# One pool for the eight PSUM banks, score halves placed on their own, and new lists for three engines

## The chip, the core and the metric

The kernel runs on one core of one Trainium2 chip. The metric is the device time of one execution in microseconds (us). Each kernel is built once and run several times; one more execution is profiled, and its rows are what this document reads. TensorE is called PE, VectorE DVE, ScalarE ACT, GpSimd POOL and SyncE SP, as in the profile. PE writes only to PSUM, which has eight banks of 512 fp32 values per partition; ACT and DVE read it.

## The reference

The input is q, k and v with 8 batches, 8 heads, 576 positions and 64 values per head. An attention with a window of 128 positions and a linear position bias feeds a channel mix.

```python
scores = scale * np.matmul(q, k.transpose(0, 1, 3, 2))
rel = pos[:, None] - pos[None, :]
mask = (rel >= 0) & (rel < window)                       # window = 128
scores = np.where(mask, scores + bias[None], -1e9)       # bias = -slope[head] * |rel|
attn = exp(scores - max) ; attn /= attn.sum(-1)
x = (attn @ v) as [8, 576, 512]                          # heads side by side
x_prev = x shifted by one position
xk = mu_k * x + (1 - mu_k) * x_prev
xr = mu_r * x + (1 - mu_r) * x_prev
k = np.maximum(xk @ w_k, 0.0)                            # 512 -> 1024
v = k * k @ w_v                                          # 1024 -> 512
out = sigmoid(xr @ w_r) * v
```

## The kernel before

The work is cut into blocks, one block being a run of instructions on one engine. For a batch and a pair of heads these are, in the order of the data:

- q and k are turned (transposes in `qk_quad` L1078, `halves` L837, or by a DMA), and copied from PSUM to `qk` (L696).
- `scores` (L698) multiplies k by q for the blocks that the window touches (L726, 12 matmuls with 64 rows of the array). A head pair fills two halves, `HALF0` and `HALF1`, of 2 x 512 values each. ACT takes the exponential of each half (L740) into `at`, and DVE multiplies by the mask and bias factors (L753). For the first batch the bias is added by matmuls instead (L713).
- `attend` (L759) multiplies by v (L781, 18 matmuls), DVE takes a reciprocal (L787) and scales into `xu` (L793).
- `out_t` or `out_some` turn `xu` back (L820, L837), ACT copies it to `xt` (L696), and `shift` makes xk and xr on DVE (L880, L887).

The channel mix works on pairs of batches (1152 rows) in pieces of 256 to 512 rows. For each of eight column groups a K block (L983, four matmuls) makes xk @ w_k, ACT applies relu (L990), DVE or ACT squares (L964, L962). For each 128 rows an R block (L1001, four matmuls) makes xr @ w_r, ACT takes tanh (L1008), two V blocks (L1017, four matmuls each) make the last product, DVE combines both (L1022), and SP sends the row out (L1047).

PSUM is held in six tiles. Two tiles `duo` have two banks each (class `p2`), and four tiles `uno` have one bank each (class `p1`). The two halves of a head pair's scores take the two duos together; an attend takes one duo; everything else takes an uno. A `Hold` is a claim on a buffer of a class; it is taken when a block starts in the plan and given back when its last reader has ended.

The order is not left to a scheduler. `Plan.add` collects all blocks with their dependences; the lists in `ORDER` say for PE, ACT and DVE in which order each runs its blocks, and `Plan.run` (L161) goes through the lists, hands out the buffers and emits the instructions in the order of its own start times. Below it, the tile layer puts in the semaphore waits: for every tile it keeps the order of emission between a write and the reads and writes of the same tile that conflict with it. `Plan.pick` (L130) chooses the buffer: the lowest free one for a class without pairs; for a class with pairs, a single claim takes a free bank whose partner is in use if there is one:

```python
return max(free, key=lambda a: ((a ^ 1) not in free, a))
```

Of the kernel before, what the change touches and what calls it, by code (L numbers as in the profile page):

```python
# [38 lines left out]
""".split()],  # L39
    "ACT": [int(x) for x in """  # L40
# [11 lines left out]
""".split()],  # L52
    "DVE": [int(x) for x in """
# [187 lines left out]
def kernel(  # L241
# [25 lines left out]
    W = D + 1  # L267
# [30 lines left out]
    SS = ()  # L298
# [70 lines left out]
    duo = [pst.tile([128, 2, 512], FP32, name=f"duo{i}") for i in range(2)]  # L369
    uno = [pst.tile([128, 512], FP32, name=f"uno{i}") for i in range(4)]  # L370
    N1 = 4
    PT = "p1"

    def one(h):
        return uno[h.idx if h.cls == "p1" else N1 + h.idx]

    def two(h):
        return duo[h.idx]

    plan = Plan(dict(qx=2, p2=2, p1=N1, pt=4 - N1, qk=NQ, at=NA, xu=NX, vs=NV, cb=NC, ts=2, tt=2, xt=2, dl=2, dl0=4,  # L380
                     xk=2, rl=3, kk=3, rs=4, ot=NO),
                {}, WAIT)
# [291 lines left out]
    h_mu = Hold("p1")  # L674
# [9 lines left out]
    h_wm = Hold("p1")  # L684
# [13 lines left out]
    def scores(b, g, parts, bias, hq, ha, deps, prio, need, free):  # L698

        todo, dur = [], 0.0  # L700
        for (pieces, m0, tt) in parts:
            a0 = BASE[pieces[0][0]] + pieces[0][1] - 128 * pieces[0][0]
            w = sum(n for _, _, n in pieces)
            todo.append((pieces, m0, tt, a0, w, Hold("p2")))
            dur += sum(max(n / 2400 + .0025, .03) for _, _, n in pieces)
            dur += 0.01 + (2 * mm(w) if bias else 0)
# [24 lines left out]
        s = op(PE, (0.12 if bias else 0.02) + dur, deps, prio + (2,), emit, list(need) + [x[5] for x in todo], free)  # L731
# [27 lines left out]
    def attend(b, g, t0, t1, ha, deps, prio):  # L759
# [3 lines left out]
        hp, hx = Hold("p1" if 2 * nt * W <= 512 else "p2"), Hold("xu")  # L763
# [5 lines left out]
        def a5():  # L769
            if hp.cls == "p1":  # L770
                return one(hp)[:, 0:2 * nt * W].rearrange("p (h t c) -> p h t c", h=2, c=W)
            return two(hp)[:, :, 0:nt * W].rearrange("p h (t c) -> p h t c", c=W)
# [36 lines left out]
    def out_t(b, g, t0, t1, hx, deps, prio, hk, ht, late=None):  # L809

        c0, c1 = 128 * t0, min(S, 128 * t1)
        n = c1 - c0
        hp = Hold(PT if b else "p1")

        def tp():
            return one(hp).bitcast(BF16)

        def emit(e):
            for t in range(t0, t1):
                nc.tensor.transpose(  # L820
                    tp()[:, 128 * t:128 * t + 128],
                    xu_buf[hx.idx][:, t].rearrange("p h d -> p (h d)"), ident)

        o = op(PE, 0.0565 * (t1 - t0), deps, prio + (1,), emit, [hp], [hx])
        x = op(XT(b, g), {ACT: act_t(n), DVE: dve_t(n)}, [o, virt_xt[b]], prio + (1,), lambda e: copy_any(
            e, xt_buf[ht.idx][:, g, X0 + c0:X0 + c1], tp()[:, c0:c1]), (), [hp])
        return shift(b, g, c0, c1, [x], prio, hk, ht, late)

    def halves(n, block):

        hp = [Hold("p1"), Hold("p1")]
# [75 lines left out]
    def tails_full(b, prio, htt, hs):  # L907
        hp = Hold("p1")
# [16 lines left out]
    def tails(b, prio):  # L925
# [8 lines left out]
        hp = Hold("p1")  # L934
# [33 lines left out]
    def channel_mix(P, c0, c1, first, xks, xrs, order):  # L968
# [9 lines left out]
        for fo in range(NFO):  # L978
            hp, hr = Hold("p1"), Hold("rl")
# [16 lines left out]
        for i, c in enumerate(range(c0 // 128, c1 // 128)):  # L996
            hp, hs = Hold("p1"), Hold("rs")
# [12 lines left out]
            hv, ho = Hold("p1"), Hold("ot")  # L1010
# [16 lines left out]
            for a, b in ((0, FIN), (FIN, 512)) if final else ((0, 512),):  # L1027
                if a:
                    hv = Hold("p1")
# [40 lines left out]
    def qk_quad(b, g, nr, buf, deps, prio, c0, hq, take, free):  # L1070

        hp = [Hold("p1"), Hold("p1")]
# [25 lines left out]
    for part in range(2):  # L1098
# [3 lines left out]
        for g in range(G):  # L1102
# [13 lines left out]
            hp = Hold("p1") if part == 0 else None  # L1116
# [51 lines left out]
    def mask_pe(j):  # L1168
        hp = Hold("p2")
# [55 lines left out]
    def qk_full(b, g, prio):  # L1225
        hp, hq = Hold(PT), Hold("qk")
# [101 lines left out]
```

## Time and profile before

| | before |
|---|---|
| median of 3 runs | 229.33 us (228.99 to 229.42) |
| the profiled execution's own time | 228.84 us |
| its span (first to last instruction) | 227.1 us |
| PE busy | 221.8 us (98% of the span), 2587 matmuls |
| DVE busy | 188.8 us (83%) |
| ACT busy | 155.0 us (68%) |
| POOL busy | 92.0 us (41%) |
| mean granted clock of PE | 0.998 |

The profile's page lists the busy time of each engine, the span in 40 slices with the busy tenths of each engine and the granted clock, the chain of work that ended last, and groups of equal instructions. In a group's row the number after the comma is the mean duration of one instruction in ns, and "idle before" is how long its engine stood idle just ahead of such instructions, with what released it. Durations of matmuls overlap: the next one starts well before the one before it has drained.

### The profile page before, as it was taken

How to read it: one execution, taken by the hardware profiler on the slowest of the kernel's cores; microseconds unless marked ns; L12 is line 12 of the kernel's file. 1: busy time of each engine (PE TensorE's matmuls, PEld its weight loads, DVE VectorE, ACT ScalarE, POOL GpSimd, SP SyncE). 2: the span in 40 equal slices, each digit the busy share in tenths (PEclk: the TensorE clock that was granted, in tenths of full speed). 3: DMA queues.
4: the chain of work that ended last, by engine and by line, in shares of the span. 5: the costliest groups of instructions: out<-in, count | busy, mean ns of one | idle time of the engine just before them, and what ended most of it. 6: DMA issues, size and time to landing. Idle time of an engine off the chain costs nothing.

```text
span 227.1 us, 6442 instructions
## 1 busy us (share of the span) xinstructions
PE 221.8 (98%) x2587; PEld 133.2 (59%) x2587; DVE 188.8 (83%) x423; ACT 155.0 (68%) x279; POOL 92.0 (41%) x118
## 2 busy tenths in 40 slices
PE   8899999999999999999999999999999999999994
PEld 8576766755666755556666554546765455446552
DVE  6786999899879998899978996999899988963433
ACT  0678999999989984975868358768567564047511
POOL 8856726599962964385208750240000000000000
PEclk9999999999999999999999999999999999999999
DMA  6999999999999999999999999999150415430124
GB/s 165 179 185 200 197 196 175 199 180 151 196 156 165 137 130 180 168 182 147 211 180 158 120 185 231 177 136 222 30 135 3 123 46 52 131 136 3 49 92 139
DMA packets 129981, 33.19 MB, mean 146 GB/s; under 512 B 116632, under 2 KB 126112, under 8 KB 129952
## 3 DMA queue, kind: packets, MB, share of 16 engines
q0 software_dynamic: 95728, 16.26, 97.5%
q1 hardware_dynamic: 32480, 15.94, 34.1%
q10 hardware_dynamic: 1744, 0.59, 1.1%
q8 instruction: 20, 0.33, 0.6%
q14 instruction: 9, 0.07, 0.1%
HBM read 33.56 MB, written 9.44 MB: 189 GB/s over the span
## 4 chain that ended last, share of the span: by engine, by line
PE 92%; ACT 3%; DMA 2%; SPq 1%; issue 0%; DVE 0%; DVEq 0%; ACTq 0%
PE uno L983 28%; PE uno L1017 28%; PE uno L1001 13%; PE duo L726 7%; PE duo L781 7%; DMA qx<-in_q_dram 2%; PE uno L837 2%; PE uno L1078 2%; ACT at L740 1%; PE duo L713 1%; ACT qk L696 1%; PE uno L781 1%; SPq L550 1%; PE uno L687 1%; PE uno L820 1%; PE uno L939 0%
## 5 line engine op out<-in xcount | busy, mean ns | idle before, releaser
L983 PE MATMUL uno<-xk,wk_sb 128*128 128x256 bf16 (+2 forms) x416 | 72.0, 314 | 0.1
L740 ACT ACTIVATE at<-duo 128x1024 bf16<-128x1024 f32 (+2 forms) x68 | 65.5, 985 | 8.8 <-PE duo L726 8.5
L1017 PE MATMUL uno<-wv_sb,kk 128*128 128x512 bf16 (+2 forms) x296 | 69.7, 374 | 0.0
L990 ACT ACTIVATE rl<-uno 128x256 bf16<-128x256 f32 (+2 forms) x104 | 46.4, 471 | 26.4 <-PE uno L983 21.0
L983 PEld LDWEIGHTS <-wk_sb 128*128 128x128 bf16 x416 | 38.7, 98 | 24.2 <-issue 0.3
L1017 PEld LDWEIGHTS <-kk 128*128 128x128 bf16 x296 | 27.2, 98 | 27.3
L500 POOL DMA_DIRECT2D vs<-in_v_dram x32 | 28.4, 904 | 31.8 <-PE duo L781 25.9
L753 DVE TENSOR_TENSOR at<-at,mask 128x1024 bf16<-128x1024 bf16 x56 | 36.9, 682 | 1.8 <-ACT at L740 1.8
L964 DVE TENSOR_TENSOR kk<-rl 128x256 bf16<-128x256 bf16 (+2 forms) x94 | 30.2, 339 | 8.8 <-ACT rl L990 8.4
L1008 ACT ACTIVATE rs<-uno 128x512 bf16<-128x512 f32 x36 | 21.1, 604 | 22.2 <-PE uno L1001 22.1
L1001 PE MATMUL uno<-wr_sb,xr 128*128 128x512 bf16 x144 | 36.1, 379 | 0.0
L1022 DVE SCALAR_TENSOR_TENSOR ot<-rs,uno 128x512 f32<-128x512 bf16 (+2 forms) x37 | 24.4, 666 | 10.5 <-PE uno L1017 8.8
L887 DVE SCALAR_TENSOR_TENSOR xk<-dl,mu_sb,xt 128x576 bf16<-128x576 bf16 (+1 forms) x32 | 24.4, 779 | 0.0
L887 DVE SCALAR_TENSOR_TENSOR xr<-dl,mu_sb,xt 128x576 bf16<-128x576 bf16 (+1 forms) x32 | 24.3, 776 | 0.0
L781 PEld LDWEIGHTS <-at 128*128 128x128 bf16 x576 | 21.0, 97 | 4.7 <-ACT at L740 0.4
L793 DVE TENSOR_TENSOR xu<-duo,rc 128x640 bf16<-128x640 f32 x28 | 22.6, 815 | 0.2
L1001 PEld LDWEIGHTS <-xr 128*128 128x128 bf16 x144 | 13.3, 98 | 13.5 <-issue 0.2
L531 POOL DMA_DIRECT2D cb<-in_k_dram x20 | 17.5, 888 | 6.9 <-DMA vs<-in_v_dram 4.7
L781 PE MATMUL duo<-vs,at 128*128 128x65 bf16 x448 | 18.6, 193 | 0.0
L531 POOL DMA_DIRECT2D cb<-in_q_dram x20 | 17.7, 935 | 1.2 <-PE duo L781 1.1
L696 ACT COPY xt<-uno 128x640 bf16<-128x640 bf16 (+3 forms) x28 | 15.0, 583 | 3.3 <-PE uno L837 2.5
L880 DVE TENSOR_TENSOR dl<-xt 128x576 bf16<-128x576 bf16 (+1 forms) x32 | 13.5, 432 | 2.8 <-ACT xt L696 2.7
(83 smaller groups left out, 197.9 us busy)
## 6 DMA issues: line engine op xcount, KB each, us to landing
out_dram<-ot SPq DMA_DIRECT2D x30, 256.0 KB, 4.6
vs<-in_v_dram POOLq DMA_DIRECT2D x32, 128.0 KB, 7.8
cb<-in_q_dram POOLq DMA_DIRECT2D x20, 128.0 KB, 6.3
cb<-in_k_dram POOLq DMA_DIRECT2D x20, 128.0 KB, 12.1
out_dram<-ot SPq DMA_DIRECT2D x10, 128.0 KB, 1.8
wk_sb<-in_moe_w_k_dram POOLq DMA_DIRECT2D x2, 512.0 KB, 9.1
cb<-in_q_dram POOLq DMA_DIRECT2D x4, 256.0 KB, 9.7
cb<-in_k_dram POOLq DMA_DIRECT2D x4, 256.0 KB, 8.6
```

The costliest lines, as they stand in the source:

```text
L500: return dma(POOL, 256, issue_t(1024), lambda e: nc.gpsimd.dma_start(out=vs_buf[h.idx][:, j, :, 0:D], in_=v[b, :, 128 * j:128 * j + 128].r ...
L531: return [dma(POOL, 256, issue_t(1024), lambda e, r=r: nc.gpsimd.dma_start(out=cb_buf[h.idx][:, i, r], in_=src[:, :, r]), [g], kind="q") f ...
L740: lambda e, ah=ah, w=w, hp=hp: nc.scalar.activation(out=ah(), in_=two(hp)[:, :, 0:w], func=AF.Exp, scale=float(scale)), (), [hp])
L753: nc.vector.tensor_tensor(out=a, in0=a, in1=m, op=ALU.mult)
L781: nc.tensor.matmul(a[:, hl, t - t0], lhsT=at[:, lo:lo + 128], rhs=vs[:, u, 2 * g + hl, 0:W] if u < NF else tvb[:, 2 * g + hl, 0:W], start= ...
L887: lambda e: nc.vector.scalar_tensor_tensor(out=buf[hk.idx][:, g, e0 + c0:e0 + c1], in0=dls(), scalar=mu[:, g:g + 1], in1=xc(1), op0=ALU.mu ...
L964: nc.vector.tensor_tensor(out=out, in0=in_, in1=in_, op=ALU.mult)
L983: nc.tensor.matmul(one(hp)[:, 0:n], lhsT=wk_sb[:, po, 128 * fo:128 * fo + 128], rhs=xk_buf[hx.idx][:, po, c0:c1], start=(po == 0), stop=(p ...
L990: a = op(ACT, act_t(n), [s], pr, lambda e, hp=hp, hr=hr: nc.scalar.activation(out=rl_buf[hr.idx][:, 0:n], in_=one(hp)[:, 0:n], func=AF.Rel ...
L1001: nc.tensor.matmul(one(hp), lhsT=xr_buf[hx.idx][:, po, 128 * c:128 * c + 128], rhs=wr_sb[:, po], start=(po == 0), stop=(po == NPO - 1))
L1017: nc.tensor.matmul(one(hv)[:, a:b], lhsT=kk_buf[hk.idx][:, fo, o:o + 128], rhs=wv_sb[:, fo, a:b], start=(fo == 0), stop=(fo == NFO - 1))
L1022: nc.vector.scalar_tensor_tensor(out=ot_buf[ho.idx][:, a:b], in0=rs_buf[hs.idx][:, a:b], scalar=1.0, in1=one(hv)[:, a:b], op0=ALU.add, op1 ...
```

## The change

The six PSUM tiles become four tiles of two banks, and all eight banks form one class `p`; a claim for one bank or for two neighbouring banks comes out of the same pool, and `pick` uses its rule for pairs. For batches 1 to 7 the two score halves of a head pair become two blocks (`SS = range(1, B)`, where it was empty), each with its own claim of two banks, so that PE has 68 score blocks in place of 40. The lists of PE, ACT and DVE are new throughout. POOL and SP have no lists; they follow the order in which their blocks were added. The work itself is the same.

```diff
 ORDER = {
     "PE": ...
-105 101 76 85 128 75 52 119 121 46 117 98 47 65 40 51 81 68 97 88 122 84 41 112 48 120 72 93 82 94 77 45 63 100
+39 106 68 112 113 93 63 47 96 57 110 81 105 76 123 103 124 125 54 86 79 114 128 67 100 66 92 78 115 120 72 43
 ...
-    SS = ()
+    SS = range(1, B)
 ...
-    duo = [pst.tile([128, 2, 512], FP32, name=f"duo{i}") for i in range(2)]
-    uno = [pst.tile([128, 512], FP32, name=f"uno{i}") for i in range(4)]
-    N1 = 4
-    PT = "p1"
+    duo = [pst.tile([128, 2, 512], FP32, name=f"duo{i}") for i in range(4)]
 
     def one(h):
-        return uno[h.idx if h.cls == "p1" else N1 + h.idx]
+        return duo[h.idx // 2][:, h.idx % 2]
 
     def two(h):
-        return duo[h.idx]
+        return duo[h.idx // 2]
 
-    plan = Plan(dict(qx=2, p2=2, p1=N1, pt=4 - N1, qk=NQ, ...
-                {}, WAIT)
+    plan = Plan(dict(qx=2, p=8, qk=NQ, ...
+                {"p": (0, 2, 4, 6)}, WAIT)
 ...
-            todo.append((pieces, m0, tt, a0, w, Hold("p2")))
+            todo.append((pieces, m0, tt, a0, w, Hold("p", 2)))
 ...
-        hp, hx = Hold("p1" if 2 * nt * W <= 512 else "p2"), Hold("xu")
+        hp, hx = Hold("p", 1 if 2 * nt * W <= 512 else 2), Hold("xu")
 ...
-            hp, hr = Hold("p1"), Hold("rl")
+            hp, hr = Hold("p"), Hold("rl")
```

The loop over batches 1 to 7 already had both forms of the scores; with `SS` it now takes the first:

```python
if b in SS:
    s0, (m0,) = scores(b, g, [HALF0 + (None,)], ...)
    _, (m1,) = scores(b, g, [HALF1 + (htt,)], ..., [(s0, 0.0)], ...)
else:
    _, (m0, m1) = scores(b, g, [HALF0 + (None,), HALF1 + (htt,)], ...)
```

More of the change, by code (lines that the diff above doesn't have):

```diff
@@ L368 @@
     warm = cst.tile([128, 128], BF16, name="warm")
-    duo = [pst.tile([128, 2, 512], FP32, name=f"duo{i}") for i in range(2)]
-    uno = [pst.tile([128, 512], FP32, name=f"uno{i}") for i in range(4)]
-    N1 = 4
-    PT = "p1"
+    duo = [pst.tile([128, 2, 512], FP32, name=f"duo{i}") for i in range(4)]
     def one(h):
-        return uno[h.idx if h.cls == "p1" else N1 + h.idx]
+        return duo[h.idx // 2][:, h.idx % 2]
     def two(h):
-        return duo[h.idx]
-    plan = Plan(dict(qx=2, p2=2, p1=N1, pt=4 - N1, qk=NQ, at=NA, xu=NX, vs=NV, cb=NC, ts=2, tt=2, xt=2, dl=2, dl0=4,
+        return duo[h.idx // 2]
+    plan = Plan(dict(qx=2, p=8, qk=NQ, at=NA, xu=NX, vs=NV, cb=NC, ts=2, tt=2, xt=2, dl=2, dl0=4,
                      xk=2, rl=3, kk=3, rs=4, ot=NO),
-                {}, WAIT)
+                {"p": (0, 2, 4, 6)}, WAIT)
     LAT = {PE: 0.2, ACT: 0.22, DVE: 0.16}
@@ L670 @@
         op0=ALU.mult), [n_ident], (0, 2 + h)) for h in range(H)]
-    h_mu = Hold("p1")
+    h_mu = Hold("p")
     def emit_mu(e):
@@ L682 @@
         out=mu_sb.rearrange("p i o -> p (i o)"), in_=one(h_mu)[:, 0:2 * NPO]), (), [h_mu])
-    h_wm = Hold("p1")
+    h_wm = Hold("p")
     def emit_warm(e):
@@ L730, in scores @@
             dur *= 1.6
-        s = op(PE, (0.12 if bias else 0.02) + dur, deps, prio + (2,), emit, list(need) + [x[5] for x in todo], free)
+        s = op(PE, (0.12 if bias else 0.01 * len(parts)) + dur, deps, prio + (2,), emit, list(need) + [x[5] for x in todo], free)
         s.rows = (128 if bias else 64, 64)
@@ L769, in a5 @@
         def a5():
-            if hp.cls == "p1":
+            if hp.n == 1:
                 return one(hp)[:, 0:2 * nt * W].rearrange("p (h t c) -> p h t c", h=2, c=W)
@@ L812, in out_t @@
         n = c1 - c0
-        hp = Hold(PT if b else "p1")
+        hp = Hold("p")
         def tp():
@@ L829, in halves @@
     def halves(n, block):
-        hp = [Hold("p1"), Hold("p1")]
+        hp = [Hold("p"), Hold("p")]
         def emit(e):
@@ L907, in tails_full @@
     def tails_full(b, prio, htt, hs):
-        hp = Hold("p1")
+        hp = Hold("p")
         def emit(e):
@@ L933, in tails @@
             return tails_full(b, prio, htt, hs)
-        hp = Hold("p1")
+        hp = Hold("p")
         def emit(e):
@@ L996, in channel_mix @@
         for i, c in enumerate(range(c0 // 128, c1 // 128)):
-            hp, hs = Hold("p1"), Hold("rs")
+            hp, hs = Hold("p"), Hold("rs")
             def emit3(e, c=c, hp=hp):
@@ L1009, in channel_mix @@
                 out=rs_buf[hs.idx], in_=one(hp), func=AF.Tanh, scale=0.5), [hs], [hp])
-            hv, ho = Hold("p1"), Hold("ot")
+            hv, ho = Hold("p"), Hold("ot")
             o = 128 * c - c0
@@ L1028, in channel_mix @@
                 if a:
-                    hv = Hold("p1")
+                    hv = Hold("p")
                 for half in range(2):
@@ L1070, in qk_quad @@
     def qk_quad(b, g, nr, buf, deps, prio, c0, hq, take, free):
-        hp = [Hold("p1"), Hold("p1")]
+        hp = [Hold("p"), Hold("p")]
         def emit(e):
@@ L1115 @@
                 cs = src1[g // 2]
-            hp = Hold("p1") if part == 0 else None
+            hp = Hold("p") if part == 0 else None
             def emit_t(e, part=part, g=g, hp=hp, f32=f32):
@@ L1168, in mask_pe @@
     def mask_pe(j):
-        hp = Hold("p2")
+        hp = Hold("p", 2)
         def emit(e):
@@ L1225, in qk_full @@
     def qk_full(b, g, prio):
-        hp, hq = Hold(PT), Hold("qk")
+        hp, hq = Hold("p"), Hold("qk")
         hc = ch[b]
```

84 rows, old and new, of the table ORDER are left out of this document.

## Prediction

> **What bounds the kernel now.** I read the page's busy shares and slices first, then the head of the chain of waits.
>
> ```profile
> PE 221.8 (98%) x2587; PEld 133.2 (59%) x2587; DVE 188.8 (83%) x423; ACT 155.0 (68%) x279; POOL 92.0 (41%) x118
> PE   8899999999999999999999999999999999999994
> ACT  0678999999989984975868358768567564047511
> PEclk9999999999999999999999999999999999999999
> PE 92%; ACT 3%; DMA 2%; SPq 1%; issue 0%; DVE 0%; DVEq 0%; ACTq 0%
> ```
>
> PE is busy in every slice from the second to the last but one, at full granted clock, and it makes up 92% of the chain. So the kernel takes as long as PE's list does: the time changes by what PE's blocks cost and by every stretch in which PE stands still. The next view is the list of who waited for whom (total, times, longest): the longest rows of ACT and DVE for PSUM, and both rows that PE has.
>
> ```profile
> ACT rs L1008 <- PE uno L1001: 22.1, 17, 5.4
> ACT rl L990 <- PE uno L983: 21.0, 30, 2.6
> ...
> DVE ot L1022 <- PE uno L1017: 8.8, 9, 2.6
> ...
> PE uno L687 <- DVE warm L469: 1.0, 1, 1.0
> ...
> PE uno L1123 <- DMA qx<-in_q_dram: 0.5, 1, 0.5
> ```
>
> PE waits twice, once for a memset and once for a load, and never for a reader of PSUM; ACT and DVE wait for PE. How that is possible shows in the timeline (start, length, engine and line) around 73 us:
>
> ```profile
> 72.45 0.60 PE L983 MATMUL uno<-xk,wk_sb 128*128 128x256 bf16 x4
> 72.89 1.03 PE L1001 MATMUL uno<-wr_sb,xr 128*128 128x512 bf16 x4
> 73.14 0.38 ACT L990 ACTIVATE rl<-uno 128x256 bf16<-128x256 f32 x1
> 73.42 1.13 ACT L1008 ACTIVATE rs<-uno 128x512 bf16<-128x512 f32 x2
> 73.75 1.04 PE L983 MATMUL uno<-xk,wk_sb 128*128 128x256 bf16 x8
> ```
>
> PE starts its R block at 72.89, before the K block has drained (72.45 + 0.60 = 73.05), and ACT reads the K block's bank at 73.14 while PE writes another. Reading runs beside writing.
>
> **Fewer row switches: about 1 us less.** The attention's blocks use 64 or 128 rows of the array, and PE pays for the change. In the chain:
>
> ```profile
> 99.72 0.55 PE duo L726 x12
> 100.27 0.97 PE uno L1001 x4
> 101.24 1.73 PE uno L1017 x8
> ```
>
> Four matmuls of 512 columns take 1.73 / 2 = 0.865 us behind a block of 128 rows, and 0.97 behind the 64-row scores: a switch is 0.105 us. I counted the places in the two built programs where a matmul has another row count than the one before it: 102 before, 92 after, because the new list puts halves of two head pairs and transposes side by side. That is 10 x 0.1 = 1.0 us off PE. The 28 score blocks that are split keep their matmuls (2587 in both programs), their 68 exponentials and 56 masks, so the cut itself adds nothing but places where PE may switch, and those are in the count.
>
> **Edits at nothing.** Four squares go from DVE to ACT, and so does one q/k copy.
>
> ```profile
> L962 ACT ACTIVATE kk<-rl 128x256 bf16<-128x256 bf16 x9 | 3.6, 428 | 0.0
> L696 ACT COPY qk<-uno 128x512 bf16<-128x512 bf16 x19 | 10.6, 599 | 0.0
> ```
>
> This is 4 x 0.43 + 0.60 = 2.3 us more on ACT, which is free for 227 - 155 = 72 us. If none of it were covered it would cost those 2.3 us.
>
> **The pool: waits between the two banks of a pair.** This is the large term. Before, each single bank is a tile of its own. After, two banks are halves of one tile, and the waits are put in by tile. I read the instruction lists of both built programs with the instruction that each wait names. In the changed one PE waits 84 times for an ACT or DVE instruction that reads only the *other* bank of the pair (62 and 22 times), and ACT and DVE wait 82 times for a matmul that writes only the other bank (59 and 23). The program before has no such wait. And pairs are shared as a rule, since the pool's `pick` prefers a bank whose partner is in use, and the claims of one bank are the majority.
>
> What one costs: a case from the new PE list, about three fifths down, is an R block on bank 7, a K block of 512 columns on bank 6, an R block on bank 7. The K block is emitted ahead of the first tanh, so tanh waits for K though it reads the other bank; the second R block needs bank 7 and waits for tanh. PE stands still for K's drain, tanh, and two hand-overs. The rows, with relu for the other pairs of blocks:
>
> ```profile
> L990 ACT ACTIVATE rl<-uno 128x256 bf16<-128x256 f32 x48 | 17.9, 392 | 9.3 <-PE uno L983 7.7 <-DVE kk L964 0.9 <-DVE ot L1022 0.4
> L990 ACT ACTIVATE rl<-uno 128x512 bf16<-128x512 f32 x24 | 14.0, 600 | 11.1 <-PE uno L983 8.8 <-issue 1.7 <-DVE kk L964 0.5
> L1008 ACT ACTIVATE rs<-uno 128x512 bf16<-128x512 f32 x36 | 21.1, 604 | 22.2 <-PE uno L1001 22.1
> L1022 DVE SCALAR_TENSOR_TENSOR ot<-rs,uno 128x512 f32<-128x512 bf16 x35 | 23.6, 680 | 9.6 <-PE uno L1017 7.9 <-DMA out_dram<-ot 0.8 <-ACT rs L1008 0.6
> ```
>
> The drain is 1.03 - 0.865 = 0.165 us (timeline and chain above). A hand-over from PE to a reader is, for the K block above, 73.14 - 73.05 = 0.09 at most; over the reads that waited for PE the trace gives 0.04 as the median. A reader's release of PE is not shown before, as PE never waits for one; I take 0.05 us and keep 0 to 0.1. The case then costs 0.165 + 0.04 + 0.604 + 0.05 = 0.86 us where it cost nothing. With PE work on another pair between, it costs that much less.
>
> How many cost how much, from both sides:
>
> - *Lower end.* For each PE block that waits for a reader, I took drain, hand-overs and the reader's row, and subtracted the PE work that stands in the list between the block that releases the reader and the waiting one. What is left over zero comes to 14.3 us at 40 places after, 0.6 us at 5 places before: +13.7. Here a reader starts the moment PE lets it; ACT and DVE have no queue.
> - *Upper end.* Each of the 84 waits pays a relu or tanh in full: 84 x (0.165 + 0.04 + 0.60 + 0.05) = 72 us.
> - *Value taken.* ACT and DVE run in order, so an ACT instruction that waits for the other bank's matmul holds what is queued behind it: the exponentials and relus for which the next PE blocks wait. I followed the three lists from front to back, each instruction with its row's mean, PE blocks at their distances in the trace with 0.1 per switch, each starting when its engine is free and all its waits are over. Before's lists end at 224.2 us this way, and in the trace the last DVE row ends at 224.0; PE stands 3.2 us. After's lists end at 255.4; PE stands 34.9 us at 84 places, the longest 1.25, in all parts of the run. That is +31.8 idle, and the end moves by 255.4 - 224.2 = +31.2 with the switches in it. With hand-overs of 0.1 it is +33.6. This lies nearer to the lower end, as many of the 84 waits find a reader that is long done.
>
> What is late next: loads of v, q and k are issued by POOL when an attend has freed their buffer, so they come later with PE and stay ahead of it; SP's row stores follow DVE the same way.
>
> **Sum.** The profiled execution takes 228.84 us, 1.7 over its span. 228.84 + 31.2 = 260.0; the median of the runs is 0.5 above the profiled one: 260.5 us.
>
> **Rivals.**
>
> *The waits are met before PE comes to them, and only the switches count.* For it: ACT is free for 32% of the span, and the new lists were laid out for eight banks, more than the four single ones that were there. It decides if PE's new list leaves 0.86 us or more of other work between the two uses of a pair at nearly all of the 84 places; at 40 it doesn't. Price: the followed lists with these waits left out, 224.2 down to 223.6, or the 1.0 us of the switches: 227.8 in the profiled execution, 228.3 us as a median, faster than before. The Trainium skill's page "PSUM — Partial Sum Buffer", section "PSUM bank collisions raise a hardware error", says that two engines on different banks run clean, so that a guard by bank is enough; the timeline at 73.14 agrees. By that rule alone the time would be this rival's. But the waits stand in the program, whatever the chip would allow. Chance 0.05; another 0.02 for a time within 0.2% of before, which is about what a measurement of this kernel can tell from no change.
>
> *Only the direct shortfalls bite.* The queue on ACT makes up its delays, as its free third suggests: 228.84 - 1.0 + 13.7 + 0.5 = 242 us. Against it: ACT's slices read 9 in the second fifth of the run, where there is nothing to make up with. Chance 0.10.
>
> *The clock falls.* With PE stopping 84 times the granted clock may drop:
>
> ```profile
> 20.00:60.00 40.00, 39.85 (x713) 26.05 (x713) 37.42 (x82) 38.84 (x78) 28.78 (x36) 1.00 1.82 188
> ```
>
> In this stretch (from the windows; second number PE's busy time, third from last the clock) PE stands 0.15 us and has clock 1.00. At half clock its 39.85 us would double: 260.5 + 39.85 = 300 us. Against it: the longest stop that I find is 1.25 us, and PE then goes on for about 3 us on average (255 / 84). The Trainium skill's page "TensorE: Matmul & The Clock Gate", section "A second HAM failure mode: psum-queue depth-cycling", tells of just such short stops between groups of matmuls that make the clock swing; the table of its section "Why this matters for your kernels" puts the danger at gaps over about 3 us. No trace here shows a stop of either kind. Chance 0.03.
>
> **The numbers.** Forecast 0.80, direct shortfalls 0.10, met waits 0.05, clock 0.03, no change 0.02. The forecast's own range is the range: 250 (followed lists with a third of the stops too many: 31.2 x 2/3 = 21) to 272 (hand-overs of 0.1, and a quarter more for the loads and stores that I took as punctual: 33.6 x 1.25 = 42). The other cases lie outside and hold 0.20 together. Faster 0.05, within 0.2% 0.02, slower 0.93.
>
> **What would show it.** Right: in the list of waits PE gets rows "PE duo ... <- ACT" for L990, L1008, L696 and L1022, tens of microseconds together; PE's busy share falls to about 87% with nearly the same busy time; the chain gains ACT and DVE; granted clock stays near 1. The switches: L1001 or L1017 groups behind scores less often at 0.97. Wrong: PE still at 97% (the waits are covered), or a granted clock well under 1 (then the clock, not the readers), or a time near 242 with ACT as busy as before but PE idle only at the direct places.

## Result and the profile after

The changed kernel takes 259.67 us (median of 4 runs, 259.62 to 260.40). The kernel before takes 229.16 us (median of 4 runs, 228.96 to 229.42). The ratio is 1.134, with a 95% interval of 1.131 to 1.136: 30.5 us slower. The forecast was 260.5 us.

The page of the changed kernel: busy time (share of the span) and instructions, three rows of slices, and the chain that ended last.

```profile
span 257.5 us, 6437 instructions
PE 229.0 (89%) x2587; PEld 133.7 (52%) x2587; DVE 189.6 (74%) x418; ACT 157.8 (61%) x284; POOL 92.4 (36%) x118
...
PE   8898878879997899899999897799889999899893
...
ACT  2679679689795785684387734684465844224510
...
PEclk9999999999999999999999999999999999999999
...
PE 66%; ACT 16%; DVE 12%; issue 4%; DMA 1%; ACTq 0%; DVEq 0%
```

The matmuls are the same 2587, at the same granted clock. PE's slices, solid 9s before, are now mixed with 7s and 8s, and 28% of the chain is ACT and DVE, which held 3% before. ACT has five instructions more and is still idle for 100 us: PE doesn't wait because ACT is full. The list of waits (total, times, longest), first rows for PE:

```profile
PE duo L982 <- ACT rl L989: 3.3, 6, 0.7
PE duo L982 <- ACT rs L1007: 2.8, 5, 1.1
PE duo L836 <- ACT rs L1007: 2.3, 3, 0.9
PE duo L1000 <- ACT rs L1007: 1.5, 3, 0.7
PE duo L1016 <- ACT rs L1007: 1.3, 2, 0.7
PE duo L982 <- ACT qk L695: 1.0, 2, 0.8
PE duo L686 <- DVE warm L468: 1.0, 1, 1.0
PE duo L1016 <- DVE ot L1021: 1.0, 2, 0.7
```

Before, PE had two rows here, 1.5 us together, and neither named a reader of PSUM. Now the rows sum to 24.7 us in 49 waits: ACT ends 37 of them (18.5 us), DVE 12 (6.2 us, with the old 1.0 us for `warm`). That the PE rows name K blocks (L982) waiting for a tanh (L1007) is the mark of the change: before, no list of waits had such a row.

The account closes. The span grew by 257.5 - 227.1 = 30.4 us. Of that, 24.7 - 1.5 = 23.2 us are listed waits, and 229.0 - 221.8 = 7.2 us are PE busy time for the same matmuls. The likely reading is that a block's drain, once hidden under the next block, now stands by itself: 7.2 / 0.165 is about 44 drains, and the list has 47 waits more than before.

The case that the prediction worked by hand, R block on bank 7, K on bank 6, R on bank 7, in the timeline (start, length, engine and line, idle time before and its releaser in brackets):

```profile
159.00 1.03 PE L1000 MATMUL duo<-wr_sb,xr 128*128 128x512 bf16 x4
...
160.06 0.60 ACT L989 ACTIVATE rl<-duo 128x512 bf16<-128x512 f32 x1 [1.17 <-PE duo L1000]
160.71 1.02 PE L982 MATMUL duo<-xk,wk_sb 128*128 128x512 bf16 x4 [0.69 <-ACT rl L989]
...
161.77 0.60 ACT L1007 ACTIVATE rs<-duo 128x512 bf16<-128x512 f32 x1 [1.11 <-PE duo L982]
162.42 1.02 PE L1000 MATMUL duo<-wr_sb,xr 128*128 128x512 bf16 x4 [0.69 <-ACT rs L1007]
```

Tanh (L1007) wants the R block that was drained at 160.03, but starts at 161.77, when the K block beside it has drained. PE's next R block wants the bank that tanh frees, and starts at 162.42. From the K block to the R block are 1.71 us, for 0.86 us of matmuls: PE stands for the other 0.85. Both of PE's waits here are for readers of the very bank that PE wants next. New is what holds these readers: relu (L989, bank 6) waits for the R block on bank 7, tanh (bank 7) for the K block on bank 6. PE and ACT take turns where they worked side by side before.

### The profile page after: what moved, and what is told of

Its sections match the earlier page's. It is cut to its first block, busy times and chain, and to the rows that moved or that the text cites. A ratio compares the mean times of both kernels' runs of the same rounds, so it can differ in the third digit from the quotient of the medians.

```text
span 257.5 us, 6437 instructions
## 1 busy us (share of the span) xinstructions
PE 229.0 (89%) x2587; PEld 133.7 (52%) x2587; DVE 189.6 (74%) x418; ACT 157.8 (61%) x284; POOL 92.4 (36%) x118
## 4 chain that ended last, share of the span: by engine, by line
PE 66%; ACT 16%; DVE 12%; issue 4%; DMA 1%; ACTq 0%; DVEq 0%
PE duo L1016 22%; PE duo L982 21%; PE duo L1000 10%; PE duo L780 5%; ACT rl L989 5%; ACT rs L1007 4%; PE duo L725 3%; ACT at L739 3%; DVE ot L1021 2%; ACT xt L695 2%; ACT qk L695 2%; DVE qk L695 2%; PE duo L1077 1%; DVE at L752 1%; PE duo L836 1%
## 5 line engine op out<-in xcount | busy, mean ns | idle before, releaser
L982 PE MATMUL duo<-xk,wk_sb 128*128 128x256 bf16 (+2 forms) x416 | 72.4, 313 | 8.6 <-ACT rl L989 3.3
L989 ACT ACTIVATE rl<-duo 128x256 bf16<-128x256 f32 (+2 forms) x104 | 45.5, 470 | 53.9 <-PE duo L982 25.7
L1016 PE MATMUL duo<-wv_sb,kk 128*128 128x512 bf16 (+2 forms) x296 | 70.2, 373 | 3.8 <-ACT rs L1007 1.3
L982 PEld LDWEIGHTS <-wk_sb 128*128 128x128 bf16 x416 | 39.3, 97 | 35.4 <-issue 14.1
L1000 PE MATMUL duo<-wr_sb,xr 128*128 128x512 bf16 x144 | 36.3, 379 | 3.0 <-ACT rs L1007 1.5
L1021 DVE SCALAR_TENSOR_TENSOR ot<-rs,duo 128x512 f32<-128x512 bf16 (+2 forms) x37 | 24.5, 665 | 16.3 <-PE duo L1016 6.6
L1007 ACT ACTIVATE rs<-duo 128x512 bf16<-128x512 f32 x36 | 21.2, 597 | 24.9 <-PE duo L1000 7.0
L792 DVE TENSOR_TENSOR xu<-duo,rc 128x640 bf16<-128x640 f32 (+2 forms) x36 | 26.6, 743 | 0.4
L780 PE MATMUL duo<-vs,at 128*128 128x65 bf16 x512 | 22.2, 193 | 0.0
L695 ACT COPY xt<-duo 128x512 bf16<-128x512 bf16 (+3 forms) x28 | 15.6, 579 | 4.3 <-PE duo L836 1.1
L786 DVE RECIPROCAL rc<-duo 128x10 f32<-128x10 f32 (+2 forms) x36 | 7.5, 209 | 11.7 <-PE duo L780 8.9
```

The source lines that it names most:

```text
L695: (nc.scalar.copy if e == ACT else nc.vector.tensor_copy)(out=out, in_=in_)
L780: nc.tensor.matmul(a[:, hl, t - t0], lhsT=at[:, lo:lo + 128], rhs=vs[:, u, 2 * g + hl, 0:W] if u < NF else tvb[:, 2 * g + hl, 0:W], start= ...
L982: nc.tensor.matmul(one(hp)[:, 0:n], lhsT=wk_sb[:, po, 128 * fo:128 * fo + 128], rhs=xk_buf[hx.idx][:, po, c0:c1], start=(po == 0), stop=(p ...
L989: a = op(ACT, act_t(n), [s], pr, lambda e, hp=hp, hr=hr: nc.scalar.activation(out=rl_buf[hr.idx][:, 0:n], in_=one(hp)[:, 0:n], func=AF.Rel ...
L1000: nc.tensor.matmul(one(hp), lhsT=xr_buf[hx.idx][:, po, 128 * c:128 * c + 128], rhs=wr_sb[:, po], start=(po == 0), stop=(po == NPO - 1))
L1007: lambda e, hp=hp, hs=hs: nc.scalar.activation(out=rs_buf[hs.idx], in_=one(hp), func=AF.Tanh, scale=0.5), [hs], [hp])
```

## Experiments

**The tiles alone.** Lists, claims and blocks of before; only the four single banks become halves of two tiles.

```diff
-    uno = [pst.tile([128, 512], FP32, name=f"uno{i}") for i in range(4)]
+    duet = [pst.tile([128, 2, 512], FP32, name=f"duet{i}") for i in range(2)]
+    uno = [duet[i // 2][:, i % 2] for i in range(4)]
```

> The kernel before with its lists, claims and classes untouched; only the four single banks are now the halves of two two-bank tiles, so no block moves. Theory (waits between the banks of one tile): slower, by more than the change itself, as the lowest-numbered banks 0 and 1 are used most and now share a tile: 82 PE waits for a reader of the other bank are in the program (59 on ACT, 23 on DVE); the three lists followed with the row means end 44.9 us later, so about 274 us. PE busy share near 84%. Rival A (the new lists or the split cost the time): no change, 229 us. Rival B (the common pool, which puts more blocks in flight and picks other banks, costs it): no change, 229 us.

273.59 us, ratio 1.195 (1.191 to 1.198). A line of the page, two of the waits, and the timeline of one such wait:

```profile
PE 232.0 (85%) x2587; PEld 135.8 (50%) x2587; DVE 191.4 (70%) x423; ACT 157.4 (58%) x279; POOL 92.0 (34%) x118
```
```profile
PE duet L984 <- ACT rl L991: 8.0, 14, 0.9
PE duet L984 <- ACT rs L1009: 3.1, 5, 0.8
```
```profile
99.46 1.03 PE L984 MATMUL duet<-xk,wk_sb 128*128 128x512 bf16 x4
...
100.59 0.69 DVE L1023 SCALAR_TENSOR_TENSOR ot<-rs,duet 128x512 f32<-128x512 bf16 x1 [0.79 <-ACT at L741]
...
100.84 0.19 PE L727 MATMUL duo<-tt 64*128 64x64 bf16 x2
...
101.31 0.60 ACT L991 ACTIVATE rl<-duet 128x512 bf16<-128x512 f32 x1 [1.49 <-DVE ot L1023]
...
101.96 1.02 PE L984 MATMUL duet<-xk,wk_sb 128*128 128x512 bf16 x4 [0.92 <-ACT rl L991]
```

No instruction was added or moved, a relu of 512 columns takes 599 ns (600 before), and the banks are used as before; 44 us came with the names of the tiles. Of the 34.8 us that PE waits, all but 1.0 stand before blocks that write `duet`, as they must if sharing is the cause.

The stop at 101.96 shows more than the text so far has told. The K block of 99.46 and its relu use bank 0 of the shared tile, `ot` and the next K block bank 1. In the built program `ot` waits for the first K block, relu waits for `ot`, and the second K block waits for relu: each for work on the other bank. The middle wait stands between two instructions that both only read PSUM: the tile layer orders readers on ACT and DVE as well, not only reads against writes. Relu starts at 101.31, 0.03 us after `ot` ends and 0.8 after its own K block has drained (100.49). The built programs have 40 such waits between readers of different banks here, 22 in the change, and none before.

So neither the lists, nor the split, nor the pool is needed for the loss.

**One shared tile in place of two.**

```diff
-    uno = [pst.tile([128, 512], FP32, name=f"uno{i}") for i in range(4)]
+    duet = pst.tile([128, 2, 512], FP32, name="duet")
+    uno = [duet[:, 0], duet[:, 1]] + [pst.tile([128, 512], FP32, name=f"uno{i}") for i in range(2, 4)]
```

> As the run with two shared tiles, but only banks 0 and 1 share one; banks 2 and 3 are tiles of their own. Theory: between before and the run with two shared tiles; 49 PE waits for a reader of the other bank are left (37 on ACT, 12 on DVE), the followed lists end 32.1 us later: about 261 us. Rivals A and B: no change, 229 us.

260.72 us, ratio 1.138 (1.135 to 1.140). In this kernel the lowest free single bank is handed out first, so banks 0 and 1 are used most, and in the built program PE has 49 waits between two banks of one tile where two shared tiles gave 82. The cost per wait is 31.3 / 49 = 0.64 us here and 44.2 / 82 = 0.54 us there: the loss follows the number of such waits, not quite in proportion. By the stops that the traces list (46 and 61) it is 0.68 and 0.72 us a stop, which is closer.

**The pool alone.** The changed kernel's four two-bank tiles and claims, with before's lists and unsplit scores.

```diff
 ORDER = {
+    (the lists of before)
...
-    SS = range(1, B)
+    SS = ()
```

> One pool of eight banks in four two-bank tiles as in the change, but with the lists of the kernel before and the two score halves of a head pair in one block. Theory: slower like the change or more, since the old lists have 102 row switches and put the pairs' banks just as close: 80 PE waits for a reader of the other bank; the followed lists end 40.4 us later, about 270 us. Rival A (new lists or split): 229 us. Rival B (the pool): also about 260 us, but then the run with only the tiles shared stays at 229.

269.25 us, ratio 1.174 (1.171 to 1.177). The new lists and the split are worth 269.25 - 259.67 = 9.6 us on shared tiles: the trace lists 59 waits of PE (31.1 us) with the old lists, 49 (24.7 us) with the new. They aren't what costs.

**Eight tiles of one bank.** The changed kernel with its lists, split, pool and `pick`; every bank is a tile. A read over two banks can't name two tiles, so it is cut in two (68 more exponentials, 28 more reciprocals, 28 more scalings).

```diff
-    duo = [pst.tile([128, 2, 512], FP32, name=f"duo{i}") for i in range(4)]
+    bank = [pst.tile([128, 512], FP32, name=f"bank{i}") for i in range(8)]
     def one(h):
-        return duo[h.idx // 2][:, h.idx % 2]
+        return bank[h.idx]
     def two(h):
-        return duo[h.idx // 2]
+        return bank[h.idx], bank[h.idx + 1]
...
-    nc.scalar.activation(out=ah(), in_=two(hp)[:, :, 0:w], ...)
+    [nc.scalar.activation(out=ah()[:, hl], in_=two(hp)[hl][:, 0:w], ...) for hl in range(2)]
```

> The changed kernel with its pool, lists and split, but each of the eight banks is a tile of its own. What reads two banks is cut in two: 68 more exponentials on ACT and 28 more reciprocals and 28 more scalings on DVE; none of the 84 PE waits for another bank is left. Theory: the time falls back to 232 us, 2.7 us over before, because ACT and DVE have more instructions (the followed lists end at 226.9 against 224.2). Rival A (lists or split): stays near 259 us or rises, as the waits were not what cost. Rival B (the pool): stays near 259 us.

231.22 us, ratio 1.009 (1.006 to 1.012). Page, chain and PE's waits:

```profile
PE 223.2 (97%) x2587; PEld 133.1 (58%) x2587; DVE 190.2 (83%) x474; ACT 159.5 (69%) x352; POOL 92.3 (40%) x118
...
PE 92%; ACT 4%; DVE 2%; issue 1%; DVEq 0%; ACTq 0%
```
```profile
PE bank L1088 <- issue: 1.5, 2, 0.9
PE bank L686 <- DVE warm L468: 1.0, 1, 1.0
PE bank L1133 <- DVE qk L695: 0.9, 1, 0.9
PE bank L993 <- ACT rl L1000: 0.3, 1, 0.3
```

Same order, same banks, and 28.4 of the 30.5 us are gone, though ACT and DVE have more to do. The rows "PE <- ACT rs" are gone with them.

**What the lists and the pool are worth without shared tiles.** Three more kernels: before's banks and lists with the same cut reads, the pool with before's lists on eight tiles, and the kernel with after's lists again beside them.

```diff
-    duo = [pst.tile([128, 2, 512], FP32, name=f"duo{i}") for i in range(2)]
+    bank = [pst.tile([128, 512], FP32, name=f"bank{i}") for i in range(4)]
```

> The kernel before with its two two-bank tiles cut into four tiles of one bank, and each exp, reciprocal and scaling that reads two banks cut into one per bank (the same cuts as in the changed kernel with eight tiles of one bank, which took 231.22 us). Lists and claims of banks are those of before. The three lists followed with the row means end at 225.4 us, 1.2 above before: expected 230.5 us. If the cuts are what costs 1.9 us there, this kernel is 0.3 to 0.7 us below that one; a rival, that the new lists themselves cost that, puts this one at 229.3.

> The pool for all eight banks with the lists of before (each head pair's score halves at one place, as before), every bank a tile of its own, two-bank reads cut in two. Followed, the lists end at 225.7 us: expected 230.8 us, within 0.4 us of before's banks with the same cuts. Against the same pool in four two-bank tiles (269.25 us) the 38 us go. A rival, that a pool brings conflicts over banks whatever the tiles, puts it above 240 us.

> The changed kernel with eight tiles of one bank once more, to stand beside before's banks with the same cuts on one chip: 231.2 us, of which 0.5 to 0.7 us above the kernel with before's lists and the same cuts, although the array switches its rows ten times less (1.0 us by the step of the prediction). A rival, that the ten switches are a clear gain, puts this one below it.

Measured: 229.72 us (ratio 1.0015, 1.0003 to 1.0027), 230.17 us (1.0043, 1.0028 to 1.0059) and 231.25 us (1.0091, 1.0071 to 1.0110). The pool on separate tiles costs 0.45 us: 39 us of the pool's loss hang on the tiles. The cuts cost 0.5 us, less than the 1.2 that I expected. The new lists cost 1.1 us more than before's on the same pool, and 1.5 more than before's banks. I had written 0.5 to 0.7, from a followed end set against a measured time; the followed ends themselves, 226.9 and 225.4, differ by the 1.5 measured. The ten switches that the new lists save don't show as a gain; the likely reason is that PE stands longer elsewhere. The windows of 20 to 60 us (second number PE's busy time), of before's banks with cut reads and then of after's lists:

```profile
20.00:60.00 40.00, 39.27 (x720) 25.91 (x724) 37.48 (x89) 39.23 (x97) 28.73 (x36) 1.00 1.86 189
```
```profile
20.00:60.00 40.00, 38.08 (x690) 25.46 (x690) 35.16 (x83) 38.01 (x96) 28.73 (x36) 1.00 1.85 184
```

PE is idle for 0.7 us in the one and 1.9 in the other (1.4 in the repeat). The spans differ by 2.1 us (1.0 in the repeat), so more than half of that lies in this stretch, in which ACT is nearly full. The first trace and the repeat's lack some 30 matmul records each, so their idle times are upper bounds.

**The split alone.** Before's tiles and lists, the two halves of a head pair as separate blocks next to each other.

```diff
-    SS = ()
+    SS = range(1, B)
```

> Before's six tiles (two of two banks, four of one) and before's lists, with the two score halves of a head pair made separate items that stand next to each other in the list. Nothing changes in what waits for what; followed, the list ends at 224.2 us as before: expected 229.3 us, no change. A rival, that placing the halves on their own costs something by itself (other waits in the built program), would show 1 us or more.

229.18 us, ratio 1.0003 (0.9992 to 1.0013). Placing the halves on their own costs nothing by itself.

**The price of a row switch.** That split, with the block of 128 rows that stood just ahead of a head pair's two halves moved between them, for 22 pairs.

```diff
 ORDER["PE"]:
-    ... K S0 S1 ...
+    ... S0 K S1 ...
```

> The kernel before with its score halves as separate items (229.18 us), in which 22 blocks of 128 rows (K, R or V) that stood just ahead of two score halves now stand between them. The same instructions; the array changes its row count 44 times more. By the prediction's 0.1 us a switch that is 4.4 us; the lists followed with the row means give 224.2 to 229.0, of which 4.2 are switches at 0.096 and 0.6 standing: expected 234.0 us. A rival, that a switch costs nothing and the 0.97 of the chain has another reason, gives 229.2 to 229.8.

234.28 us, ratio 1.022 (1.020 to 1.024): 5.1 us more than the split alone, which ran on another chip, and 4.9 more than before on the same chip (229.39). Two pieces of its chain, four matmuls of 512 columns each, the first behind a score half, the second behind 128 rows:

```profile
121.11 0.97 PE uno L1019 x4
...
123.06 0.86 PE uno L1019 x4
```

With the 0.6 us that PE stands longer by the followed lists taken off, 4.5 / 44 = 0.10 us a switch. The trace's list shows no such growth in PE's waits (2.0 us, 2.4 for the split alone); without that deduction it is 5.1 / 44 = 0.12. The rival (a switch is free) falls. The Trainium skill's page "TensorEngine Tiling (Array Packing)", section "Key Properties", says that a change of tiling mode drains the array. The sign agrees; a whole drain as the timeline shows it (0.165 us) would have been 7.3 us for 44, and the run took 5.1.

## Why the prediction was right

- *PE's list bounds the kernel.* Right: where PE's standing was taken away (eight tiles), PE is busy for 97% of the span again, and the time went back to within 2 us of before.
- *The pool's waits between banks, +31.2 us.* Right in mechanism and size: 30.4 us in the span, shown by taking the sharing alone in (+44 us) and out (-28 us). It names waits between a reader and a matmul; the 22 between two readers it doesn't name, though lists followed with all waits of the program hold them too. Its hand-overs were taken as 0.04 us from PE to a reader and 0.05 back. The chain around the worked case shows 0.02 and 0.04:

```profile
159.16 0.88 PE duo L1000 x4
160.04 0.02 issue
160.06 0.61 ACT rl L989
160.67 0.04 issue
160.71 1.04 PE duo L982 x4
```

  So the case cost 0.85 us where 0.86 was written. In the chain of the whole run all 34 steps from ACT to PE show 0.04, and 24 of 25 from PE to ACT 0.02: hand-overs of 0.1 throughout, as the upper end of the range has them, don't occur. That end adds up to 229.3 + 42 = 271.3 and not 272, which changes nothing.
- *Places.* PE was followed to 84 stops of 34.9 us; the trace lists 49. The sum holds because the trace seems to count drains as busy: against before, the followed lists have 34.9 - 3.2 = 31.7 us more standing, the trace 23.2 of listed waits and 7.2 of busy time, 30.4 together. For the same reason PE's share fell to 89% and not 87%, with 7 us more busy time and not "nearly the same". I mixed up two ways of counting one stop. The 84 waits for a reader of the other bank aren't a list of the stops either: in the case worked by hand PE waits for readers of its own bank.
- *The rows named.* L989, L1007, L695 and L1021 are there, 5.9, 7.9, 4.0 (ACT's copies) and 2.0 us over all of PE's rows for them: 20 us, the lower edge of "tens". L1021 runs on DVE, not on ACT as the prediction has it.
- *The switches, -1.0 us.* The price of one is shown (0.10 us). That the ten saved would show in the time is not: on separate tiles the new lists are 1.1 us slower than before's. In the forecast this did no harm, since the followed end held both.
- *Edits at nothing.* Not tried by themselves. ACT is idle for 100 us, and the changed kernel with eight tiles has the same edits: together with the new lists they make the 1.1 us by which it stands above the same pool with before's lists.
- *Rivals.* The waits are not met by other work: 259.67, not 228. Direct shortfalls alone, 242 us, leave out 18 us. That sum has the case worked by hand in it, but lets every reader start the moment PE lets it; the relu at 101.31 in the run with the tiles alone, held for 0.8 us by `ot`, shows one kind of delay that it leaves out. How the 18 us divide among such delays is not shown. The clock didn't fall. The window of the busiest stretch, where PE stands 6.9 of 40 us, has clock 1.00 (third number from the end):

```profile
20.00:60.00 40.00, 33.10 (x649) 22.77 (x648) 29.81 (x65) 32.13 (x69) 29.17 (x36) 1.00 1.89 182
```

  The oscillation that the Trainium skill's page "TensorE: Matmul & The Clock Gate" tells of in "A second HAM failure mode: psum-queue depth-cycling" doesn't occur here, with 49 stops of at most 1.1 us. The danger that the table in its section "Why this matters for your kernels" puts at gaps over about 3 us stays untested: no run here has such a gap.

No version beat the kernel before. The best of these, the split on before's tiles, is level with it.

## What to carry to other kernels

What a tile covers is part of the schedule: where waits are put in by tile, two banks in one tile are one resource: a reader of one holds the writer of the other, a writer holds the reader, and a reader on ACT holds one on DVE and the other way round. Share a tile between banks only for blocks that use both, and give single banks tiles of their own, even if some reads must be cut in two: here the cuts cost 0.5 us and sharing cost 28 to 44. Before trusting a new order, look in the built program for waits whose two instructions touch different banks, and follow the lists with measured row means; that gave the end within 1 us in all four kernels with shared tiles.

## What the runs showed of the hardware

The hand-over from PE's drain to a reader is 0.02 us and from a reader back to PE 0.04 us in the chain of the changed kernel, less than I had assumed; the profile models the ends of matmuls, so the first of these is only as good as that model. The granted clock stays at 1.00 through 49 stops of up to 1.1 us. A change between 64 and 128 rows costs PE 0.10 to 0.12 us.
